# Sending turned attention features to DRAM one pipeline round later, fetching them further ahead, and a denser interleave in a two-layer linear-attention kernel

## The chip, the cores and the metric

The kernel runs on one core of a Trainium2 chip. The metric is the device time of one execution in microseconds (us). Engines are named as in the profile: PE is TensorE (PEld its weight loads), DVE is VectorE, ACT is ScalarE, POOL is GpSimd, and SP is SyncE, whose instructions here are almost all DMA issues; "SPq" is SP's instruction queue, which is worked off in order.

## The reference

Four blocks are applied in turn to x of 2048 rows by 576 columns: attention A, dense B, attention A, dense B, each with a layer norm in front and a residual around it.

```python
qkv = x @ wqkv                                   # 32 heads of 18 columns
phi_q = concat(softmax(q @ w_phi), softmax(-(q @ w_phi)))      # phi_k alike, per head
kv  = einsum("bhsf,bhsd->bhfd", phi_k, v);  z = einsum("bhsf->bhf", phi_k)
o   = einsum("bhqf,bhfd->bhqd", phi_q, kv) / (einsum("bhqf,bhf->bhq", phi_q, z) + 1e-6)
A(x) = o @ wo
B(x) = relu(x @ w1 + b1)**2 @ w2 + b2            # hidden size 4608
```

## The kernel before, in words

**Tiles.** The 2048 rows are four blocks of 512 rows, each of four row tiles t = 0..3 of 128. The hidden size is 36 slices f of 128. Every matmul operand is split into a high and a low part, and a product is three matmul groups (high by high, low by high, high by low).

**Stages of a layer.** After the key sums are known, a barrier stage computes the attention output of the first block in `order`. Then the dense part of `order[0]` runs as `g_mlp` while the attention of later blocks is woven in (first weave); then the dense part of `order[1]` runs as `g_mlp` with more attention woven in (second weave); then the last two blocks are done together by `g_pair`. In layer 0 `order` is 3, 2, 0, 1, in layer 1 it is 1, 0, 3, 2. In the profile names lose their buffer numbers: `m_3` and `m_2` are the two dense stages of layer 0, `m_1` and `m_0` those of layer 1; `a_2`, `a_0`, `a_1` and `a_3` are the attention of blocks 2, 0, 1 and 3.

**The dense stage.** For each f, `first(f)` loads a slice of w1 (tile `r1`, lines 1159 and 244) and of w2 (tile `r2`, line 1161), two buffers each, and splits them on ACT, DVE and POOL (lines 1167, 1168, 1171, 1174, 1175). `hidden(f)` (line 1190, 14 matmuls), `square(f)` (lines 1197 to 1200) and `second(f)` (lines 1217 and 1208, 15 matmuls) follow. The loop body for f issues `first(f+1)`, `hidden(f)`, `square(f)`, `second(f-1)` and then yields; with two yields ahead of the loop there are 36 yields.

**The weave.** At each yield of the dense stage, `weave` adds a rate to a credit and lets the other generator run steps while the credit is at least 1; each step yields its cost, which is taken off. So rate and costs say beside which f a step is traced. The order of tracing gives priorities only: a planner then lays down a fixed order for each engine, taking the first instruction in priority that it holds to be ready. `chained` keeps each woven step's work on DVE, ACT and POOL behind that of the step before, and `held` puts it behind the newest `square`; neither holds SP.

**The woven attention.** `g_features` makes query features: a software pipeline over t of `start`, exponential, `add`, `factors`, scaling (line 853) and `turn`. `turn` transposes tile t in blocks of 32 by 32 on DVE (line 897) and at once issues four stores to a DRAM tile (`..ft`, line 900, 144 KB each). `g_out` fetches groups of the turned features back (`fetch`, line 928, five groups of up to 504 KB; all four t must have landed), splits them (lines 941 and 942), multiplies them (line 964), multiplies by wo and adds the residual (lines 999 and 1004), and normalizes (lines 459 to 534). The first two groups are fetched right ahead of the first splitting step; each later one two groups ahead. The first weave's generator is `back_first`: features of `order[1]`, queries of `order[2]`, `g_out` of `order[1]` with the features of `order[2]` inside, and the norm of `order[1]`, whose result the second dense stage reads. The second weave's is `back_second`: `g_out` of `order[2]`, queries, features and `g_out` of `order[3]`, and a prelude for `g_pair`.

Of the kernel before, what the change touches and what calls it, by code (L numbers as in the profile page):

```python
# [15 lines left out]
NT = TB // P  # L16
# [5 lines left out]
def layers_kernel(  # L22
# [79 lines left out]
    def drain(gen):  # L102
        for _ in gen:
            pass

    def weave(main, other, rate, behind=None):

        due = 0.0
        for _ in main:
            due += rate  # L110
            while due >= 1.0:
                cost = next(other, other)
                if cost is other:
                    break
                due -= cost or 1.0
        with tc.issue_after(dense[behind]) if behind else nullcontext():
            drain(other)

    def pipeline(n, stages, costs):

        for i in range(n + len(stages) - 1):
            for k in reversed(range(len(stages))):
                if 0 <= i - k < n:
                    stages[k](i - k)
                    yield costs[k]
# [9 lines left out]
    def traced_on(engine):  # L135
        return next(i for i in reversed(nc.cur_bb.bb.instructions) if i.engine == engine.engine)

    def chained(gen, strict=False, every=False):
        ends, engines = {}, [nc.vector.engine, nc.scalar.engine, nc.gpsimd.engine]
        if every:  # L140
            engines.append(nc.tensor.engine)
        while True:
            traced = nc.cur_bb.bb.instructions
            mark = len(traced)
            if strict and not every:
                ends[nc.tensor.engine] = [traced_on(nc.tensor)]
            with ExitStack() as behind:
                for before in ends.values():
                    for ins in before:
                        behind.enter_context(tc.issue_after(ins))  # L150
                cost = next(gen, gen)
            own = {}
            for ins in traced[mark:]:
                if ins.engine in engines:
                    own.setdefault(ins.engine, []).append(ins)
            for engine, step in own.items():
                ends[engine] = step if every else step[-1:]
            if cost is gen:
                return
            yield cost  # L160
# [65 lines left out]
    dense = {"v": 0}  # L226
# [413 lines left out]
    def soft_parts(src, name, apart=False):  # L640
        if apart:
            e = sb.tile([P, 2 * D], F32R, tag="hb", name=f"{name}e").bitcast(F32)
            e = e.rearrange("p (s d) -> p s d", s=2)
        else:
            e = sb.tile([P, 2, D], F32, tag="E", name=f"{name}e", bufs=4)
        v = src.rearrange("p (h d) -> p h d", d=DH)
        mm = sb.tile([P, 2, H], F32, tag="mm", name=f"{name}m")
        nc.vector.tensor_reduce(mm[:, 0], v, op=ALU.max, axis=AX.X)
        nc.vector.tensor_reduce(mm[:, 1], v, op=ALU.min, axis=AX.X)
        e4 = e.rearrange("p s (h d) -> p s h d", d=DH)  # L650
        m = mm.unsqueeze(3).to_broadcast([P, 2, H, DH])
        dense["parted"] = nc.vector.tensor_sub(e4[:, 0], v, m[:, 0])
        dense["parted", 1] = nc.gpsimd.tensor_sub(e4[:, 1], m[:, 1], v)
        return e

    def soft_exp(e):
        return nc.scalar.activation(e, e, AF.Exp)

    def soft_sums(e, name):
        r = sb.tile([P, 2, H], F32, tag="r", name=f"{name}r", bufs=4)  # L660
        nc.vector.tensor_reduce(r, e.rearrange("p s (h d) -> p s h d", d=DH), op=ALU.add, axis=AX.X)
        nc.vector.reciprocal(r, r)
        return r
# [142 lines left out]
    def held(gen, keys=("last",)):  # L806

        while True:
            with ExitStack() as behind:
                for key in keys:  # L810
                    behind.enter_context(tc.issue_after(dense[key].ins))
                cost = next(gen, gen)
            if cost is gen:
                return
            yield cost
# [15 lines left out]
    def phi_products(layer, e, name):  # L831
        zb = sums[layer]["zb"]
        ms = [sb.tile([P, D], F32, tag="qk", name=f"{name}{s}", bufs=5) for s in range(2)]
        for s in range(2):
            (nc.gpsimd if s else nc.vector).tensor_mul(ms[s], e[:, s], zb[:, s])
        return ms

    def phi_sums(ms, name):
        u = sb.tile([P, 2, H], F32, tag="u", name=name)
        for s in range(2):  # L840
            nc.vector.tensor_reduce(u[:, s], ms[s].rearrange("p (h d) -> p h d", d=DH), op=ALU.add, axis=AX.X)
        return u

    def phi_factors(u, r):
        nc.vector.tensor_mul(u, u, r)
        nc.vector.scalar_tensor_tensor(u[:, 0], u[:, 0], DEN_EPS, u[:, 1], op0=ALU.add, op1=ALU.add)
        nc.vector.reciprocal(u[:, 1], u[:, 0])
        nc.vector.tensor_mul(r, r, u[:, 1].unsqueeze(1).to_broadcast([P, 2, H]))

    def phi_scale(e, r, which=(0, 1)):  # L850
        for s in which:
            e3 = e[:, s].rearrange("p (h d) -> p h d", d=DH)
            dense[f"scaled{s}"] = (nc.gpsimd if s else nc.vector).tensor_mul(
                e3, e3, r[:, s].unsqueeze(2).to_broadcast([P, H, DH]))
# [24 lines left out]
    def g_features(layer, raws, ph, name):  # L879

        rs, ms = {}, {}

        def start(t):
            ph.append(soft_parts(raws[t], f"{name}Q{t}"))

        def add(t):
            rs[t] = soft_sums(ph[t], f"{name}Q{t}")
            ms[t] = phi_products(layer, ph[t], f"{name}m{t}")

        def factors(t):  # L890
            phi_factors(phi_sums(ms.pop(t), f"{name}u{t}"), rs[t])

        turned[name] = home = dram.tile([2 * D, TB], F32, name=f"{name}ft")

        def turn(t):
            flat = ph[t].rearrange("p s d -> p (s d)")
            nc.vector.transpose(flat, flat)
            for i in range(NQ):
                at = t * P + 32 * i
                nc.sync.dma_start(home[:, at : at + 32].rearrange("(j f) r -> f j r", f=32),  # L900
                                  flat[32 * i : 32 * i + 32].rearrange("f (j r) -> f j r", r=32))

        yield from held(pipeline(NT, (start, lambda t: soft_exp(ph[t]), add, factors, lambda t: phi_scale(ph[t], rs[t]),
                                      turn), (2.6, 0.4, 3.0, 2.8, 1.2, 1.6)), ("last", "squared"))

    def g_out(layer, b, ph, dst, name, parts=1, pause=None, behind=None, norm=None, mid=None, costs=(None, None), o_first=None):

# [14 lines left out]
        def fetch(k):  # L922
            if k < NG:
                g, w = groups[k], gw[groups[k]]
                raws[g] = sb.tile([P, 2 * D], F32, tag="E", name=f"{name}w{g}", bufs=4)[:w, : 2 * TB]
                raws[g] = raws[g].rearrange("p (s n) -> p s n", s=2)
                src = turned[name].rearrange("(s d) n -> d s n", s=2)
                nc.sync.dma_start(raws[g], src[g * GW : g * GW + w])
# [84 lines left out]
        if parts == 1:  # L1013
            for k in range(2):
                fetch(k)
        xs_of = []
        if pause:
            product, total, factors, rescale = pause
# [41 lines left out]
        begin, scale, main, rest = next(g_norm(xs_of.__getitem__, dst, f"{name}n", None, None))  # L1060
# [760 lines left out]
    for b in range(NB - 1):  # L1821
# [6 lines left out]
              ready=lambda: qpair.extend(wpair("q", "t0", TAGS_B))))  # L1828

    order = [NB - 1, NB - 2] + list(range(NB - 2))  # L1830
    b, prev = order[0], order[1]
    x, xprev = xT[b], xT[prev]
    for layer in range(2):
        ready, raws = barrier(layer, b, prev, x, xprev, kes, vpair, qpair)
        spare["tags"] = []
        early, operands, rows, nxt, keep = [], {}, [], {}, {}
        prelude, products, seconds = g_pair(layer, order[2:], operands, rows, f"m{layer}_p")

        def back_first():
            m, later = f"a{layer}_{order[2]}", []  # L1840
            mid = (g_queries(layer, order[2], None, later, m), g_features(layer, later, early, m))
            yield from g_attend(layer, order[1], None, raws, nxt, f"a{layer}_{order[1]}", dense, None, mid)
# [80 lines left out]
                if last:  # L1923
                    keep.update(x=xk, es=es, v=wpair("v", f"w{m}"))

        weave(g_mlp(layer, order[0], ready, [], f"m{layer}_{order[0]}", dense.pop("rest")), chained(back_first()), 3.7, "rows")
        back = chained(back_second())

        def then():
            drain(back)  # L1930
            next(products)

        weave(g_mlp(layer, order[1], nxt, [], f"m{layer}_{order[1]}", None, then), back, 5.0)
        back = iter(()) if layer else chained(back_keys(), True)
        for k, _ in enumerate(products):
            if k == NP - 1:
# [6 lines left out]
        if layer == 0:  # L1943
# [18 lines left out]
            order = [b, prev] + order[:2]  # L1962
# [22 lines left out]
```

## Time and profile before

| | us |
|---|---|
| Median of 3 runs | 2440.58 (2440.19 to 2441.8) |
| The profiled execution's own time | 2441.59 |
| Its span, first to last instruction | 2439.9 |
| DVE, ACT, POOL busy | 1560.5, 1289.7, 940.6 |
| Mean granted TensorE clock | 0.998 |

Read it from the busiest engine. Where one engine is busy for nearly the whole span, the time can only fall where that engine sits idle or runs at a lower clock, so the view of its waits matters most; the order of time on the engines around such a place then says who was late, and for whom that one waited.

### The profile page before, as it was taken

What the parts mean: (1) busy time and instruction counts of PE and PEld (TensorE: products, weight loads), DVE (VectorE), ACT (ScalarE), POOL (GpSimd) and SP (SyncE); (2) the same over time, 40 slices, a digit from 0 to 9 for tenths busy, and PEclk for the clock granted to TensorE, in tenths of its full rate; (3) what the DMA queues carried; (4) which work ended last, traced back from release to release, by engine and by line L of the source; (5) the groups of instructions that cost most, each with busy time, mean ns of one, the idle gap of its engine ahead of it and who ended that gap; (6) DMA issues with size and microseconds to landing.
All of it is one profiled execution on the core that took longest, in us unless ns stands there. A gap on an engine that the chain in (4) does not pass through costs nothing. (4 is left out here: it accounts for less than half of the span.)

```text
span 2439.9 us, 41475 instructions
## 1 busy us (share of the span) xinstructions
PE 2410.0 (99%) x14806; PEld 2137.9 (88%) x14806; DVE 1560.5 (64%) x2537; ACT 1289.7 (53%) x2543; POOL 940.6 (39%) x1121
## 2 busy tenths in 40 slices
PE   9999999999999999999999999999999999999999
PEld 8999888888888888888999988888887888888898
DVE  8779847664867655545766787486557675555443
ACT  4344555444456666664443444554455466676643
POOL 4555303212335565542433442032222455565321
PEclk9999999999999999999999999999999999999999
DMA  9124573666654533338753156537667444333364
GB/s 338 64 84 165 163 194 97 151 202 220 155 173 136 157 99 115 109 104 302 257 188 139 59 173 143 168 96 186 191 233 158 141 142 145 118 103 116 110 199 130
DMA packets 370646, 379.40 MB, mean 155 GB/s; under 512 B 142886, under 2 KB 270790, under 8 KB 367878
## 3 DMA queue, kind: packets, MB, share of 16 engines
q1 hardware_dynamic: 369180, 375.37, 51.2%
q8 instruction: 116, 1.90, 0.3%
q10 hardware_dynamic: 1258, 1.37, 0.2%
q14 instruction: 92, 0.75, 0.1%
HBM read 297.22 MB, written 79.41 MB: 154 GB/s over the span
## 5 line engine op out<-in xcount | busy, mean ns | idle before, releaser
L1507 POOL TENSOR_TENSOR m_ps<-m_pr,m_ps 128x128 fp32r<-128x128 f32 x144 | 98.6, 685 | 337.8 <-ACT m_ps L1505 310.7
L1506 DVE TENSOR_TENSOR m_ps<-m_pr,m_ps 128x448 fp32r<-128x448 f32 x144 | 99.8, 693 | 175.9 <-ACT m_ps L1504 175.8
L1549 PE MATMUL m_pacc<-m_ps,m_phb 128*128 128x448 f32 x864 | 185.6, 363 | 0.0
L1549 PEld LDWEIGHTS m_pacc<-m_ps,m_phb 128*128 128x128 f32 x864 | 161.9, 188 | 15.0
L1549 PE MATMUL m_pacacc<-m_ps,m_phc 128*128 128x448 f32 x648 | 147.1, 365 | 0.0
L1504 ACT ACTIVATE m_ps<-m_pr 128x448 fp32r<-128x448 f32 x144 | 82.8, 575 | 115.7 <-issue 64.9
L1549 PEld LDWEIGHTS m_pacacc<-m_ps,m_phc 128*128 128x128 f32 x648 | 119.2, 188 | 7.7
L1190 PE MATMUL m_0ph<-a_0nh,m_0h 128*128 128x512 f32 (+1 forms) x380 | 96.7, 382 | 1.6 <-ACT m_0hr L1197 1.4
L1190 PE MATMUL m_1ph<-t1onh,m_1h 128*128 128x512 f32 (+1 forms) x380 | 96.2, 381 | 2.0 <-ACT m_1hr L1197 1.8
L1217 PE MATMUL m_2acc<-m_2s,m_2hb 128*128 128x448 f32 x432 | 95.2, 367 | 2.9 <-ACT m_2s L1168 2.6
L1190 PE MATMUL m_3ph<-t0onh,m_3h 128*128 128x512 f32 (+1 forms) x380 | 96.1, 381 | 1.8 <-ACT m_3hr L1197 1.6
L1217 PE MATMUL m_0acc<-m_0s,m_0hb 128*128 128x448 f32 x432 | 95.0, 367 | 2.9 <-ACT m_0s L1168 2.6
L1190 PE MATMUL m_2ph<-a_2nh,m_2h 128*128 128x512 f32 (+1 forms) x380 | 96.6, 382 | 0.8 <-ACT m_2hr L1197 0.6
L1217 PE MATMUL m_3acc<-m_3s,m_3hb 128*128 128x448 f32 x432 | 94.2, 364 | 2.0 <-ACT m_3hb L1198 1.4
L1217 PE MATMUL m_1acc<-m_1s,m_1hb 128*128 128x448 f32 x432 | 94.2, 364 | 2.0 <-ACT m_1hb L1198 1.4
L1217 PEld LDWEIGHTS m_2acc<-m_2s,m_2hb 128*128 128x128 f32 x432 | 81.8, 190 | 11.7 <-ACT m_2s L1168 3.0
L1217 PEld LDWEIGHTS m_0acc<-m_0s,m_0hb 128*128 128x128 f32 x432 | 81.5, 190 | 11.7 <-ACT m_0s L1168 3.0
L1217 PEld LDWEIGHTS m_3acc<-m_3s,m_3hb 128*128 128x128 f32 x432 | 80.4, 188 | 10.6 <-ACT m_3hb L1198 2.1
L1217 PEld LDWEIGHTS m_1acc<-m_1s,m_1hb 128*128 128x128 f32 x432 | 80.4, 188 | 10.5 <-ACT m_1hb L1198 2.1
L1175 POOL TENSOR_TENSOR m_3s<-m_3r,m_3s 128x128 fp32r<-128x128 f32 x36 | 22.9, 637 | 161.9 <-ACT m_3s L1169 153.3
L1175 POOL TENSOR_TENSOR m_1s<-m_1r,m_1s 128x128 fp32r<-128x128 f32 x36 | 22.8, 635 | 162.0 <-ACT m_1s L1169 151.8
L1190 PEld LDWEIGHTS m_1ph<-t1onh,m_1h 128*128 128x128 f32 x380 | 68.8, 188 | 17.4 <-ACT m_1hr L1197 3.0
(2464 smaller groups left out, 7237.0 us busy)
## 6 DMA issues: line engine op xcount, KB each, us to landing
m_pr<-in_B_w SPq DMA_DIRECT2D x144, 288.0 KB
m_pr<-in_B_w SPq DMA_DIRECT2D x72, 256.0 KB
hd<-m_pu SPq DMA_DIRECT2D x72, 256.0 KB
m_pg<-hd SPq DMA_DIRECT2D x72, 256.0 KB
m_3r<-in_B_w SPq DMA_DIRECT2D x36, 288.0 KB
m_2r<-in_B_w SPq DMA_DIRECT2D x36, 288.0 KB
m_1r<-in_B_w SPq DMA_DIRECT2D x36, 288.0 KB
m_0r<-in_B_w SPq DMA_DIRECT2D x36, 288.0 KB
```

The costliest lines, as they stand in the source:

```text
L1175: nc.gpsimd.tensor_sub(s2[:, FC + P : FC + 2 * P], r2[:, R:], s2[:, FC : FC + P].bitcast(F32))
L1190: dense["hidden"] = nc.tensor.matmul(ph[:, cols], a, m, start=(k == 0), stop=(k == len(ops) - 1))
L1217: nc.tensor.matmul(acc[t][:, :R], a[:, rows], m, start=(f == 0 and k == 0), stop=(f == NF - 1 and k == 2))
L1504: nc.scalar.activation(s2[:, RO : RO + R], r2[:, :R], AF.Copy)
L1506: nc.vector.tensor_sub(s2[:, RO + R : RO + 2 * R], r2[:, :R], s2[:, RO : RO + R].bitcast(F32))
L1507: nc.gpsimd.tensor_sub(s2[:, FC + P : FC + 2 * P], r2[:, R:], s2[:, FC : FC + P].bitcast(F32))
L1549: nc.tensor.matmul(accs[b][t][:, :R], a[:, rows], m, start=(g == 0 and k == 0), stop=(g == NF - 1 and k == 2))
```

## The change

Three things are changed. The four stores of a tile leave `turn` and become a seventh stage of the features' pipeline, `store`, with a cost of 0.2, so that tile t's are issued at the head of the next round, ahead of `turn(t+1)`; those of the last tile come after a further step of cost 4.0. In `g_out`, a step of cost 3.0 follows the first two fetches. The rates of the two weaves go from 3.7 to 3.9 and from 5.0 to 5.1. No instruction is added or removed.

```diff
         def turn(t):
             flat = ph[t].rearrange("p s d -> p (s d)")
             nc.vector.transpose(flat, flat)
+
+        def store(t):
+            flat = ph[t].rearrange("p s d -> p (s d)")
             for i in range(NQ):
                 at = t * P + 32 * i
                 nc.sync.dma_start(home[:, at : at + 32].rearrange("(j f) r -> f j r", f=32),
                                   flat[32 * i : 32 * i + 32].rearrange("f (j r) -> f j r", r=32))

-        yield from held(pipeline(NT, (start, lambda t: soft_exp(ph[t]), add, factors, lambda t: phi_scale(ph[t], rs[t]),
-                                      turn), (2.6, 0.4, 3.0, 2.8, 1.2, 1.6)), ("last", "squared"))
+        def steps():
+            yield from pipeline(NT, (start, lambda t: soft_exp(ph[t]), add, factors, lambda t: phi_scale(ph[t], rs[t]),
+                                     turn, lambda t: t < NT - 1 and store(t)), (2.6, 0.4, 3.0, 2.8, 1.2, 1.6, 0.2))
+            yield 4.0
+            store(NT - 1)
+            yield 0.2
+
+        yield from held(steps(), ("last", "squared"))
...
         if parts == 1:
             for k in range(2):
                 fetch(k)
+            yield 3.0
...
-        weave(g_mlp(layer, order[0], ready, [], f"m{layer}_{order[0]}", dense.pop("rest")), chained(back_first()), 3.7, "rows")
+        weave(g_mlp(layer, order[0], ready, [], f"m{layer}_{order[0]}", dense.pop("rest")), chained(back_first()), 3.9, "rows")
...
-        weave(g_mlp(layer, order[1], nxt, [], f"m{layer}_{order[1]}", None, then), back, 5.0)
+        weave(g_mlp(layer, order[1], nxt, [], f"m{layer}_{order[1]}", None, then), back, 5.1)
```

## The prediction, made before the changed kernel ran

> **What bounds the kernel now.** I read the page first, then the waits of PE, then the order of time on SP and DVE around the longest of them, then busy time by windows.
>
> ```profile
> span 2439.9 us, 41475 instructions
> ...
> PE 2410.0 (99%) x14806; PEld 2137.9 (88%) x14806; DVE 1560.5 (64%) x2537; ACT 1289.7 (53%) x2543; POOL 940.6 (39%) x1121
> ```
>
> PE is busy 2410.0 of 2439.9 us. The change takes no matmul away, so it can gain only from the 29.9 us of idle time and from stretches at a lower clock. PE's waits, longest first (total, times, longest):
>
> ```profile
> PE m_2acc L1217 <- ACT m_2s L1168: 2.6, 1, 2.6
> PE m_0acc L1217 <- ACT m_0s L1168: 2.6, 1, 2.6
> PE m_1ph L1190 <- ACT m_1hr L1197: 1.8, 3, 0.8
> PE m_3ph L1190 <- ACT m_3hr L1197: 1.6, 2, 0.8
> PE m_3acc L1217 <- ACT m_3hb L1198: 1.4, 1, 1.4
> PE m_1acc L1217 <- ACT m_1hb L1198: 1.4, 1, 1.4
> PE m_0ph L1190 <- ACT m_0hr L1197: 1.4, 1, 1.4
> PE a_2pn L964 <- ACT a_2fh L941: 1.1, 1, 1.1
> ```
>
> All lie in the dense stages with woven attention: m_3 and m_1 are first weaves, m_2 and m_0 second weaves. Two waits of 2.6 us are for a slice of w2 split too late (m_2s, m_0s). They cost more than they show: right behind each, the granted clock (third column from the right) falls to half for 3.4 us, which is 1.7 us of lost matmul time.
>
> ```profile
> 659.80:663.20 3.40, 3.10 (x9) 2.64 (x9) 1.03 (x2) 0.78 (x2) 1.42 (x2) 0.50 1.39 224
> ...
> 1868.10:1871.50 3.40, 3.40 (x10) 2.97 (x9) 0.63 (x1) 0.78 (x2) 0.70 (x1) 0.50 1.17 192
> ```
>
> [...] The rows show the drop after 2.6 us, so I count it.
>
> Why the slice was late, in SP's queue ahead of the first of these waits:
>
> ```profile
> 639.04 2.38 SPq L900 DMA_DIRECT2D a_1ft<-a_1Q0e  x4
> 649.43 2.33 SPq L900 DMA_DIRECT2D a_1ft<-a_1Q1e  x4
> 651.86 0.59 SPq L1161 DMA_DIRECT2D m_2r<-in_B_w  x1
> 655.15 2.30 SPq L900 DMA_DIRECT2D a_1ft<-a_1Q2e  x4
> 657.55 0.61 SPq L1161 DMA_DIRECT2D m_2r<-in_B_w  x1
> 658.25 3.26 SPq L900 DMA_DIRECT2D a_1ft<-a_1Q3e  x4
> 661.56 0.71 SPq L1159 DMA_DIRECT2D m_2r<-in_B_w  x1
> ```
> ```profile
> 638.94 0.57 DVE L1174 TENSOR_TENSOR m_2s<-m_2r,m_2s 128x448 fp32r<-128x448 f32 x1
> ...
> 648.04 1.36 DVE L897 STREAM_TRANSPOSE a_1Q1e<-a_1Q1e 128x1152 f32<-128x1152 f32 x1
> ```
>
> The w2 buffer was free at 638.94 + 0.57 = 639.5 us. Its next load went out at 651.86, 12.4 us later: SP had the stores of tile 1 ahead of it and stood at them until DVE's turn ended at 648.04 + 1.36 = 649.4. Stores that wait for DVE hold up weights that wait for nothing. SP's own waits say the same of the other places:
>
> ```profile
> SPq L900 <- DVE a_0Q1e L897: 20.4, 2, 10.7
> SPq L900 <- DVE a_2Q1e L897: 16.0, 2, 9.7
> ```
>
> And in the first weave of layer 0, where the w1 slice (L1159) was wanted:
>
> ```profile
> 288.56 1.44 DVE L1171 TENSOR_TENSOR m_3h<-m_3r,m_3h 128x640 fp32r<-128x640 f32 x1 [0.55 <-DMA m_3r<-in_B_w]
> ```
> ```profile
> 297.56 2.36 SPq L900 DMA_DIRECT2D a_2ft<-a_2Q1e  x4
> 300.02 0.58 SPq L1161 DMA_DIRECT2D m_3r<-in_B_w  x1
> 304.30 2.30 SPq L900 DMA_DIRECT2D a_2ft<-a_2Q2e  x4
> 306.64 0.66 SPq L1159 DMA_DIRECT2D m_3r<-in_B_w  x1
> ```
>
> The w1 buffer was free at 290.0, its load left at 306.64, behind tiles 1 and 2. That is 16.6 us of lead gone, over two iterations of the dense stage; the 1.4 us wait of m_3acc follows.
>
> **The change, part by part.** *The stores, one round later.* Added up from the costs, as yield of 36 before and after. First weave: turns of tiles 0 to 3 at 8, 11, 12, 13, now 8, 10, 12, 12; their stores were at the turns' yields, now 10, 12, 12, 14. Second weave: turns 15, 16, 17, 18, now 15, 17, 18, 18; stores now 17, 18, 18, 20. So tile 1's stores, the worst blockers, fall behind the weight loads of one or two further slices in the planner's priority; tile 2's hardly move (same yield as the turn); tile 3's fall two yields back. The 16 issues of about 0.6 us (2.30 to 3.26 per four) stay on SP, which has room, and are moved past the weight loads only. The tiles they read are held longer, but the next user of these buffers is the fetch, which must wait for the stores in any case: nothing new.
>
> What it is worth: both 2.6 us waits with their half clock, 2 x (2.6 + 1.7) = 8.6 us. I take all of it, since a load 12.4 us earlier leaves nothing to wait for. In the first weaves the 1.4 us waits and the 0.8 us waits (two in each layer), 1.4 + 2 x 0.8 = 3.0 us per layer: bounds 0 and 6.0, and I take half, 3.0, because tile 2's stores stay in the way.
>
> *The fetch 3.0 ahead.* It goes to yield 21 (was 19) in the second weave, its first splitting step to 21 or 22 (was 20). The two waits behind the fetch, 1.4 (m_0ph) and 1.1 (a_2pn), are ACT standing at loads that have left but not landed, at a time when the DMA engines (second column from the right) are full:
>
> ```profile
> 1850.00:1856.00 6.00, 6.00 (x29) 5.22 (x28) 6.00 (x8) 2.47 (x4) 2.98 (x2) 1.00 0.26 43
> ...
> 1872.00:1876.00 4.00, 4.00 (x20) 3.55 (x19) 1.36 (x2) 1.52 (x3) 0.75 (x1) 1.00 0.92 256
> ```
>
> While SP stood at tile 1 the share was 0.26, afterwards 0.92: the same bytes, bunched. The change spreads them. Bounds 0 and 2.5; I take half, 1.2.
>
> *The rates.* The first weave gets 12.6 units of cost more (twice 4.8 for the stores and pauses, 3.0 for the fetch) against 36 x 0.2 = 7.2 of credit. Its last norm steps move from yields 32, 33, 33, 34 to 34, 34, 35, 36: no yield is left behind the last. The second weave gets 4.8 + 2 x 3.0 = 10.8 against 3.6 and ends its prelude at 36 instead of 34; that prelude's first products come after the dense stage's epilogue, so I cost that at nothing; without that cover it is a wait for the last weight split. The first weave's end is closer:
>
> ```profile
> 496.92 0.60 PE L512 MATMUL a_2np<-ident,a_2nn 128*128 128x128 f32 x4
> ...
> 501.16 0.60 PE L512 MATMUL a_2np<-ident,a_2nn 128*128 128x128 f32 x4
> ```
>
> The last residual product ends at 496.9 and the transposes of its normalized rows start at 501.16. These 4.2 us are covered to the last by the stage's closing matmuls. The step runs this late although traced at yield 34, so moving its trace to 36 may change nothing; if the cover goes, it is up to 4.2 us and a half clock of 1.7, 5.9 per layer. A gain is excluded, since that stretch has no place in the list of waits above. Between 0 and 11.8 I take 2.0 for both layers, near the first end, by the row just named.
>
> Sum: 8.6 + 3.0 + 1.2 - 2.0 = 10.8 us. From the profiled 2441.59 that is 2430.8; the median lies 1.0 below its profiled run (2441.59 - 2440.58), so 2429.8, rounded to 2430. All listed waits and both half clocks gone, with no new cost, is 8.6 + 6.0 + 2.5 = 17.1, or 2423.5; I put the low end at 2422, since other engines' order moves as well.
>
> **The rivals.** *The stores stay where they are.* The planner goes by what it holds to be ready, not by place in the trace:
>
> ```profile
> 258.04 1.06 SPq L984 DMA_DIRECT2D a_2x<-in_A_x  x2
> ```
>
> These rows are first asked for in the norm step of yield 32, and yet were issued at 258 us, ahead of tile 1's stores at 297.56, which are traced at yield 11. If SP is free in the plan when a turn ends, its stores leave at once, whatever their priority, and the change only shifts the weave. Against it: the w1 load above, free at 290.0, was planned behind stores whose turn came later, so the planner does see a full queue there and goes by priority. Time 2440.6, give or take 2.
>
> *The transfers are the limit.* With the share at 0.92 behind the stores, loads that leave earlier may land no earlier. Then half of the 8.6 stays and the 1.2 falls away: gain 4.3 + 3.0 - 2.0 = 5.3, so 2441.6 - 5.3 - 1.0 = 2435.3. [...] Against it stands the 0.26.
>
> *The fetch takes the stores' place, and the kernel is slower.* The fetch is asked for 5.2 units after the last stores (6.6 before), and those are now the last in priority. SP then stands at the fetch until they have landed, with weight loads behind it. It decides from about 10 us of standing, what tile 1's stores show now; then each of the four weaves pays a wait such as now, 2.6 + 1.7 = 4.3, in all 17.2: 2441.6 - 10.8 + 17.2 - 1.0 = 2447. Against it: in the first weave stores and fetch lie two yields apart, and in the second the landing of the last stores took 3.32 us even among full engines, by the chain of work that ended last:
>
> ```profile
> 1868.13 3.32 DMA a_2ft<-a_2Q3e
> ```
>
>
> **How the numbers follow.** The forecast gets 0.57 (2422 to 2435), the stores staying 0.18, the transfers 0.13, the fetch 0.12. The range 2422 to 2441 holds nearly all of the first, most of the second and all of the third, about 0.8. A measurement of this kernel can tell 0.2%, 4.9 us, from no change: 2435.7 to 2445.5 is the same. Faster: 0.57 and half of the transfers, 0.64. Same: the other half and most of the second, 0.21. Slower: 0.15.
>
> **What would show it.** Right: SP's waits at L900 for a turn shrink, with the L1161 and L1159 rows ahead of the stores; the m_2s and m_0s waits of PE are gone, and no half clock near them. The second rival shows as stores in the old places among the loads; the third as a DMA share near 1 and ACT waiting for weights issued early; the fourth as a long wait at L928 with weights behind. The end of the first weave shows as a wait of the first L1190 of m_2 or m_0 for the normalized rows. I am wrong if the time is above 2436, or if the gain comes from elsewhere than the four weaves.

## The result, and the profile after

The changed kernel takes 2463.52 us (median of 4 runs, 2460.35 to 2465.5) beside 2440.67 for the kernel before on the same chip: 1.0092 times as long, 95% interval 1.0074 to 1.0109. The forecast was 2430, with 2422 to 2441 as its range. Its profiled execution took 2463.13 us. The page's head:

```profile
span 2461.4 us, 41511 instructions
...
PE 2419.7 (98%) x14806; PEld 2141.8 (87%) x14806; DVE 1566.1 (64%) x2537; ACT 1292.6 (53%) x2543; POOL 940.5 (38%) x1121
```

The span grew by 21.5 us. PE's idle time went from 29.9 to 41.7 us (11.8). Its busy time grew by 9.7 us, though it runs the same matmuls: part of the same work ran at a lower clock (mean granted clock 0.998 before, 0.996 after). Where it went, from the first matmul of each stage in both traces:

| stage | layer 0: before, after | layer 1: before, after |
|---|---|---|
| dense with first weave | 274.6, 278.9 (+4.3) | 275.1, 280.5 (+5.4) |
| dense with second weave | 297.1, 299.9 (+2.9) | 298.4, 300.2 (+1.8) |
| pair products | 316.1, 319.8 (+3.7) | 316.2, 320.4 (+4.2) |

All else together is -0.8. PE's waits after (total, times, longest); lines of the kernel stand 3 to 10 further down than before, so L900 is now L903, L928 L937, L941 L950, L1159 L1169:

```profile
PE m_ppx L1527 <- DVE m_pu L1659: 5.0, 2, 2.8
PE a_0pn L973 <- ACT a_0fh L950: 4.9, 2, 3.8
...
PE a_3pn L973 <- ACT a_3fh L950: 3.2, 1, 3.2
PE m_1ph L1200 <- ACT m_1hr L1207: 1.6, 2, 0.8
PE m_3ph L1200 <- ACT m_3hr L1207: 1.6, 2, 0.8
PE m_3acc L1227 <- ACT m_3hb L1208: 1.4, 1, 1.4
PE m_1acc L1227 <- ACT m_1hb L1208: 1.4, 1, 1.4
PE m_2ph L1200 <- ACT m_2hr L1207: 1.4, 1, 1.4
PE m_0ph L1200 <- ACT m_0hr L1207: 1.2, 1, 1.2
...
PE a_2np L512 <- DVE a_2x L1013: 0.9, 1, 0.9
```

The two 2.6 us waits for w2 are gone, as forecast, and with them the half clocks behind them. (The waits of m_2ph and m_0ph for ACT, 1.4 and 1.2, stand further on; before they were 0.6 and 1.4.) The 0.8 and 1.4 us waits of m_3 and m_1 are still in the list, as long as before. New are PE's waits for the fetched features at the start of the second weave (3.8 and 3.2, one in each layer) and for a step on the first products' accumulator at the start of the pair products (2.2 and 2.8). Windows of after around these and a third place (time, then PE, PEld, DVE, ACT, POOL busy, granted clock, DMA share, GB/s):

```profile
357.71:361.12 3.41, 2.13 (x7) 0.94 (x6) 2.50 (x4) 3.27 (x7) 0.77 (x1) 1.00 0.99 279
361.12:364.54 3.42, 3.42 (x9) 2.68 (x9) 1.60 (x3) 0.89 (x3) 0.00 (x0) 0.50 0.63 179
528.38:531.79 3.41, 0.10 (x1) 0.10 (x1) 0.64 (x1) 1.41 (x3) 0.00 (x0) 1.00 0.96 281
531.79:535.21 3.42, 3.42 (x8) 2.65 (x9) 3.32 (x6) 1.85 (x4) 0.00 (x0) 0.50 0.95 278
818.51:821.92 3.41, 1.17 (x6) 0.68 (x5) 1.95 (x4) 2.44 (x5) 2.02 (x3) 1.00 0.01 2
821.92:825.33 3.41, 3.41 (x10) 2.84 (x9) 3.41 (x10) 2.57 (x6) 0.46 (x1) 0.50 0.67 245
```

Each idle stretch of these rows is followed by 3.4 us at half clock. There are three such in each layer (in layer 1 at 1579.68, 1750.35 and 2040.48) where before had one (659.79 and 1868.10). By the clock alone that is 4 x 1.7 = 6.8 us more.

**Start of the second weave.** SP after, and two rows of SP before:

```profile
503.26 0.57 SPq L937 DMA_DIRECT2D a_0w<-a_0ft  x1
...
507.56 0.35 SPq L937 DMA_DIRECT2D a_0w<-a_0ft  x1
508.01 2.72 SPq L1288 DMA_DIRECT2D xs<-m_3x  x4
...
511.89 1.20 SPq L427 DMA_DIRECT2D a_0o0h<-wsoh  x2
...
519.34 0.38 SPq L1169 DMA_DIRECT2D m_2r<-in_B_w  x1
```
```profile
489.49 0.52 SPq L928 DMA_DIRECT2D a_0w<-a_0ft  x1
...
509.68 0.38 SPq L1159 DMA_DIRECT2D m_2r<-in_B_w  x1
```

The fifth w1 slice of the dense stage left at 519.34 in place of 509.68. Ahead of it are the last two fetches (the last at 507.56; 489.49 before), the stores of finished rows and the loads of wo, which had been spread over 20 us (489.49 to 509.68). ACT then stands at that slice:

```profile
530.38 0.74 ACT L1177 ACTIVATE m_2h<-m_2r 128x640 fp32r<-128x640 f32 x1 [4.11 <-DMA m_2r<-in_B_w]
531.03 0.61 ACT L950 ACTIVATE a_0fh<-a_0w 126x512 fp32r<-126x512 f32 x1
```

The split that PE waits for (L950) had its data; it was behind L1177 in ACT's order. PE's wait names ACT, and ACT's row names the DMA.

**Start of the pair products.** The weights of each pair of slices are split in a chain over POOL, ACT and DVE. The prelude is the split of the first pair; the splits of the second and third pair are traced with the first products. POOL's first and last step of the prelude, and first and late steps of the third pair's split, after, then before; then DVE and PE after:

```profile
784.40 1.02 POOL L1488 TENSOR_TENSOR m_ps<-m_pr,m_pr 128x384 f32<-128x384 f32 x1
...
806.87 0.53 POOL L1485 TENSOR_TENSOR m_pwb<-m_pr,m_pwb 32x128 fp32r<-32x128 f32 x1
...
811.38 1.02 POOL L1488 TENSOR_TENSOR m_ps<-m_pr,m_pr 128x384 f32<-128x384 f32 x1 [0.77 <-PE m_ppz L1527]
...
818.38 1.00 POOL L1497 TENSOR_TENSOR m_pr<-m_pr,m_ps 128x384 f32<-128x384 f32 x1
```
```profile
769.13 1.01 POOL L1478 TENSOR_TENSOR m_ps<-m_pr,m_pr 128x384 f32<-128x384 f32 x1
...
787.09 0.64 POOL L1475 TENSOR_TENSOR m_pwb<-m_pr,m_pwb 32x128 fp32r<-32x128 f32 x1
...
803.60 1.11 POOL L1478 TENSOR_TENSOR m_ps<-m_pr,m_pr 128x384 f32<-128x384 f32 x1
...
807.72 1.09 POOL L1487 TENSOR_TENSOR m_pr<-m_pr,m_ps 128x384 f32<-128x384 f32 x1
```
```profile
819.97 0.43 DVE L1483 TENSOR_TENSOR m_pwa<-m_pr,m_pwa 128x256 fp32r<-128x256 f32 x1 [2.82 <-ACT m_pwa L1482]
820.32 0.75 DVE L1659 SCALAR_TENSOR_TENSOR m_pu<-m_ppx,b1t,m_pu 128x512 f32<-128x512 f32 x1
```
```profile
817.41 1.46 PE L1227 MATMUL m_2acc<-m_2s,m_2hb 128*128 128x448 f32 x6
821.12 0.73 PE L1527 MATMUL m_ppx<-a_1nt4h,m_pwb 128*128 128x512 f32 x2 [2.24 <-DVE m_pu L1659]
```

The pair products begin 7.5 us later than before (806.3 for 798.8), but the prelude began 15.3 us later. It ended 11.1 us ahead of the first product before (787.7), and 1.1 us behind it after (807.4). The third pair's split starts at nearly the same distance from the first product in both (4.8 and 5.1 us), but after it runs among what is left of the earlier ones: its last step shown begins 7.0 us behind its first, in place of 4.1. DVE stood at a split of its result (L1483), and L1659, which frees PE's accumulator, was behind.

### The profile page after: what moved, and what is told of

It is laid out like the page before. It is cut to its first block, busy times and chain, and to the rows that moved or that the text cites. A ratio compares the mean times of both kernels' runs of the same rounds, so it can differ in the third digit from the quotient of the medians.

```text
span 2461.4 us, 41511 instructions
## 1 busy us (share of the span) xinstructions
PE 2419.7 (98%) x14806; PEld 2141.8 (87%) x14806; DVE 1566.1 (64%) x2537; ACT 1292.6 (53%) x2543; POOL 940.5 (38%) x1121
## 5 line engine op out<-in xcount | busy, mean ns | idle before, releaser
L1200 PEld LDWEIGHTS m_3ph<-t0onh,m_3h 128*128 128x128 f32 x380 | 68.8, 189 | 18.5 <-ACT m_3hr L1207 2.4
L1200 PEld LDWEIGHTS m_0ph<-a_0nh,m_0h 128*128 128x128 f32 x380 | 68.5, 190 | 16.1 <-ACT m_0hr L1207 1.6
```

Of the source, the lines that this page charges most:

```text
L1200: dense["hidden"] = nc.tensor.matmul(ph[:, cols], a, m, start=(k == 0), stop=(k == len(ops) - 1))
```

## The experiments

Times are ratios to runs of the kernel before on the same chip, as us beside 2440.7. The main theory was that the loss comes from the cost units that the change adds to the woven generators: at the rates given they let the last woven steps come 1.5 yields later in each weave, past the work that covered them. The rival was that the moved stores do it.

**e1: stores moved, without the pauses, old rates.**

```diff
-                                      turn), (2.6, 0.4, 3.0, 2.8, 1.2, 1.6)), ("last", "squared"))
+                                     turn, store), (2.6, 0.4, 3.0, 2.8, 1.2, 1.6, 0.2))
```

> The kernel before with the four stores of a tile moved to a seventh pipeline stage, also those of the last tile (one step behind its turn); no 4.0 pause, no 3.0 step after the fetch, rates 3.7 and 5.0 as before. Theory (the lost time is the added cost units, which push the tail of each weave past the work that covered it; the moved stores are good): the two 2.6 us waits for w2 and their half clocks go and none of the three new loss places appears, so 2430 to 2436 us. Rival (the moved stores themselves upset SP's queue): the new waits appear here too, 2450 to 2464 us.

1.0031 (1.0019 to 1.0043), +7.6 us: between the two ranges. None of the three new places, and the 2.6 us waits are gone, but there is no gain. PE now waits 3.9 and 4.2 us near the end of the first weaves, and 2.8 and 3.4 us for a w1 slice in the second weaves, with five windows at half clock (mean granted clock 0.997).

**e2: pauses and rates, stores in place.** Besides these lines, `yield 3.0` after the fetches and the rates 3.9 and 5.1.

```diff
-                                      turn), (2.6, 0.4, 3.0, 2.8, 1.2, 1.6)), ("last", "squared"))
+                                     turn, lambda t: None), (2.6, 0.4, 3.0, 2.8, 1.2, 1.6, 0.2))
+            yield 4.0
```

> The kernel before with its stores where they were, but with all cost units and rates of the change: 0.2 per tile and 4.0 after the features, 3.0 after the first two fetches, rates 3.9 and 5.1. Theory (cost units): the late tails appear without any moved store, about 15 us of waits and lost clock at the start of the second weave and at the start of the pair products, and the two 2.6 us waits stay: 2450 to 2465 us. Rival (the moved stores): within 4 us of 2440.

1.0077 (1.0064 to 1.009), +18.8 us: most of the 22.5, with no store moved. Its waits at the pair products are 4.5 us (5.0 in the changed kernel). Not all came as expected: the waits for the features are only 2.6 and 0.9 us, and the 2.6 us waits for w2 did not stay; 4.1 and 3.1 us for a w1 slice stand in the second weaves instead.

**e3: the change, units paid for by the rates.**

```diff
-dense.pop("rest")), chained(back_first()), 3.9, "rows")
+dense.pop("rest")), chained(back_first()), 4.08, "rows")
-None, then), back, 5.1)
+None, then), back, 5.32)
```

> The changed kernel with rates that pay for the added units in full: 4.08 in the first weave (3.7 x 136.4 / 123.8) and 5.32 in the second (5.0 x 180.8 / 170), so that the last woven steps fall on the yields of the kernel before. Theory (cost units): the waits at the start of the second weave and of the pair products go, 2432 to 2442 us. Rival (the moved stores): stays at 2455 to 2465 us.

1.002 (1.0011 to 1.003), +4.9, so 2445.6: 18 of 22.5 us are back. That lies in neither range, 4 us above the theory's and 9 below the rival's. The waits at the start of the pair products are gone. What is left lies in the first weaves (+3.4 and +3.5 us):

```profile
PE m_3acc L1227 <- ACT m_3hb L1208: 4.3, 3, 1.4
PE m_1acc L1227 <- ACT m_1hb L1208: 4.3, 3, 1.4
```

**e4: the rates alone.**

```diff
-dense.pop("rest")), chained(back_first()), 3.7, "rows")
+dense.pop("rest")), chained(back_first()), 3.9, "rows")
-None, then), back, 5.0)
+None, then), back, 5.1)
```

> The kernel before with the rates 3.9 and 5.1 alone. Theory (cost units): woven work comes up to two yields earlier, no tail is late, 2436 to 2443 us. Second rival (a denser weave by itself crowds ACT, DVE and SP): 2448 us or more.

1.0021 (1.0013 to 1.003), +5.1, so 2445.8: 3 us above the theory's range and below the rival's. Earlier is not free either.

**e5 and e6: only one weave paid,** each with one line of e3's diff: 4.08 with 5.1, and 3.9 with 5.32.

> The changed kernel with only the first weave's rate raised to pay for its added cost units, 4.08 (the second stays at 5.1). Theory (each weave's unpaid units make its own tail late): the wait at the start of the second weave goes, 3.8 us in layer 0 and 3.2 in layer 1 with 1.7 of half clock each, 10.5 in all; the wait at the start of the pair products stays, 2.2 and 2.8 us: 2450 to 2456 us. Rival (lateness runs through both weaves, the pair products' wait included, from the first): 2440 to 2448 us.

> The changed kernel with only the second weave's rate raised, to 5.32 (the first stays at 3.9). Theory (each weave's own tail): the wait at the start of the pair products goes, 2.2 and 2.8 us with 1.7 of half clock each, 8.4 in all; the wait at the start of the second weave stays: 2452 to 2458 us. Rival (it all comes from the first weave): 2460 us or more.

1.0044 (1.0032 to 1.0056) and 1.0053 (1.0038 to 1.0069): 2453.0 and 2455.1 as medians, both in the theory's range. Waits of PE in e5, then in e6:

```profile
PE m_ppx L1527 <- DVE m_pu L1659: 4.7, 2, 2.5
```
```profile
PE a_0pn L973 <- ACT a_0fh L950: 5.2, 2, 3.9
...
PE a_3pn L973 <- ACT a_3fh L950: 3.5, 1, 3.5
```

Each kernel keeps the wait of the weave that was not paid, and has lost most of the other's (in e5 the wait for L950 is 1.7 and 1.3 us). By stages, e5's pair products are as late as the change's (+3.5 and +4.4 us) and its second weaves are not (+0.2 and -3.2); in e6 the pair products are +0.1 and +1.0. The two savings, 11.8 and 9.6 us, add up to 21.4; both together (e3) gave 17.6. So each weave's tail is late by its own unpaid units.

**e7: stores issued by POOL, stores otherwise in place.**

```diff
-                nc.sync.dma_start(home[:, at : at + 32]...
+                nc.gpsimd.dma_start(home[:, at : at + 32]...
```

> The kernel before with the four stores of a tile issued by POOL instead of SP, nothing else: no store can stand ahead of a weight load in SP's queue. If the 2.6 us waits for w2 come from the stores ahead of them, as the prediction argued, they go with their half clocks: 8.6 us, 2430 to 2434 us. Rival 1 (the planner's order of other work on SP, not the stores, makes loads late; taking stores out only moves the waits): 2438 to 2450 us. Rival 2: POOL stands at the turns and its splits come late: 2445 us or more, with PE waiting for POOL's results.

1.0114 (1.0095 to 1.0133), +27.8. Rival 2's time, though not shown to be its mechanism: the 2.6 us waits are gone, and PE waits for normalized rows (3.5, 3.5, 2.7 and 2.7 us) and fetched features instead, not for POOL's results. That the waits for w2 hung on the stores fits; that freeing the loads gains time does not follow.

**e8: the 3.0 step alone; e12: 4.8 units after the features alone,** each added to the kernel before.

```diff
                 fetch(k)
+            yield 3.0
```
```diff
                                      turn), (2.6, 0.4, 3.0, 2.8, 1.2, 1.6))
+            yield 4.8
```

> The kernel before with only the 3.0 step after the first two fetches of a group, old rates. It adds 3.0 units to the first weave and 6.0 to the second (1.2 yields there). Theory (cost units): the prelude is late and PE waits at the start of the pair products, 1 to 3 us a layer and perhaps the half clock: 2443 to 2452 us, and the two 2.6 us waits stay. Rival (fetching earlier helps more than the units cost): 2436 to 2441 us.

> The kernel before with 4.8 units after the features of each block and nothing else; old rates. It adds 9.6 units to the first weave (2.6 yields) and 4.8 to the second (1.0). Theory (cost units): waits at the start of the second weave above all, 3 us or more with a half clock of 1.7 in each layer, and a smaller one at the pair products: 2450 to 2462 us. Rival: under 2445 us.

1.0027 (1.0018 to 1.0037) and 1.006 (1.0047 to 1.0073): +6.6 and +14.6, both as the theory had it in time, the places only in part. In e8 the pair products wait 1.0 us in all, there is one half clock (mean granted clock 0.999), and beside the stores 1.3 and 1.6 us (1.5 in layer 1) stand for 2.6, which was expected to stay. In e12 the loss is in the second weaves (+9.5 and +6.3 us), with 1.6 us at the first weave's last norm and seven windows at half clock in all (mean granted clock 0.995), and hardly any at the pair products; its first weaves, where 9.6 units were added, are 0.1 us longer.

**e9: all sixteen stores behind the last turn.**

```diff
+            for t in range(NT):
+                store(t)
+                yield 0.05
```

> The kernel before with all sixteen stores of a block behind the turn of its last tile, at almost no cost units, old rates. Theory (SP stands at every store whose turn is not done, and loads of weights stand behind it, whichever tile it is): SP stands once only, and the waits for weights around the stores of the second weave, 2.6 us a layer before and 2.8 to 3.4 with the stores one round later, shrink to under 1 us; 16 issues of 0.6 us in a row and a later fetch give part of it back: 2434 to 2444 us. Rival (bunching the transfers costs more than the standing): a wait of PE for the split of the fetched groups of 3 us or more in each weave, 2450 us or more.

1.0018 (1.0009 to 1.0026), +4.4: neither range. Waits for w1 beside the stores stay at 3.0 and 3.8 us; they did not shrink, and the waits of about 4 us in the first weaves are here too (4.1 and 3.9), though only 0.4 units were added there. The traced execution is the fastest of the eleven (2439.57 beside a median of 2446.11), so it does not show where the 4.4 us lie.

**e10: the changed kernel with a cheaper prelude.**

```diff
-            yield from paced(held(prelude, ("last", "squared")), 2.0)
+            yield from paced(held(prelude, ("last", "squared")), 1.0)
```

> The changed kernel with the seven steps of the prelude at 1.0 unit each in place of 2.0, nothing else. Theory (the prelude's place beside the last dense slices is what makes the pair products wait): the waits at the start of the pair products go, 2.2 and 2.8 us with 1.7 of half clock each, 8.4 in all: 2453 to 2458 us. Rival (the whole second weave is late, and the prelude's pace does not matter): 2460 to 2465 us.

1.0078 (1.0065 to 1.009), 2459.4: between. The waits at the pair products are gone, as the theory said (their stage is +0.1 and +0.7 us), and 6.5 us are lost in the second weaves in exchange (+6.0 and +5.2, where the change had +2.9 and +1.8). (Its first weaves are 2.6 and 1.6 us shorter than the change's; its mean granted clock is 0.997, the change's 0.996.) The prelude's lateness was the cause of that wait; pressing it into the same yields only moved the price.

**e11: the change in the second weaves only, paid in full.** The new stage, the pauses and the 3.0 hang on a flag that is set between the two weaves; rates 3.7 and 5.32.

```diff
+            if in_second:
+                yield 3.0
```

> The change in the second weaves only, paid in full (rate 5.32); the first weaves as in the kernel before (stores at the turn, no added units, 3.7). Theory (what is left of the loss once the units are paid lies in the first weaves, about 2 to 3.5 us each): 2437 to 2443 us. Rival (the first weave was only the place where it showed): 2445 us or more.

0.9995 (0.9986 to 1.0004): as the theory had it, no loss and no gain that can be told.

**e13 to e16: residual rows' stores issued by POOL,** on the kernel before, e1, e9 and e11.

```diff
-            nc.sync.dma_start(xm[b][t], x)
+            nc.gpsimd.dma_start(xm[b][t], x)
```

> The kernel before with the stores of the residual rows (xm) issued by POOL, behind POOL's own addition, in place of SP, where they waited 82 us in all for that addition. Theory (SP's standing costs only where a load of weights with little lead is behind it; the kernel before has no such place at these stores): 2437 to 2444 us. Rival (every standing of SP costs): under 2435 us.

> The store move alone with the residual rows' stores issued by POOL. In the store move alone, SP stood 7.2 us at one of them in each first weave with the load of a w1 slice behind it, and PE waited 3.9 and 4.2 us with half clocks. Theory (that standing is what the moved stores had become in the first weaves): those waits go, about 11 us: 2437 to 2442 us; the waits for w1 behind the turned stores in the second weaves stay. Rival (moving the stores costs for another reason): 2446 us or more.

> All sixteen stores behind the last turn, and the residual rows' stores issued by POOL. It had the same two waits of 3.9 and 4.1 us in the first weaves. Theory: they go, 2434 to 2438 us. Rival: 2443 us or more.

> The change in the second weaves only, paid in full, and the residual rows' stores issued by POOL. It had no wait at these stores' place. Theory: 2437 to 2442 us. Rival (every standing of SP costs): under 2435 us.

1.0013 (1.0004 to 1.0022), 1.0042 (1.0029 to 1.0054), 1.0014 (1.0005 to 1.0023) and 0.9992 (0.9983 to 1.0001). e13 is at the upper end of the theory's range (its median, 2444.73, 0.7 above) and e16 in it; e14 and e15 came out in their rivals'. In e14 the waits of about 4 us in the first weaves went, and others of nearly the same size came at the end of the same stages:

```profile
PE a_2po L1005 <- DVE a_2nl L521: 3.7, 1, 3.7
...
PE a_0po L1005 <- DVE a_0nl L521: 3.1, 1, 3.1
```

Taking SP's standing away there did not bring e1's loss back, so that theory fell. Left to suspect were the 0.2 units that e1 added to each tile.

**e17: e1 with the 1.6 of the turn split, so that nothing is added; e18: the change with 4.4 in the first weave.**

```diff
-                                     turn, store), (2.6, 0.4, 3.0, 2.8, 1.2, 1.6, 0.2))
+                                     turn, store), (2.6, 0.4, 3.0, 2.8, 1.2, 1.55, 0.05))
```

> The store move alone with no added cost units at all: the turn's 1.6 is split into 1.55 for the turn and 0.05 for the store (in the store move alone each tile cost 0.2 more, 1.6 units in the first weave or 0.4 yields). Theory (the move itself replaces one wait by another): 2446 to 2452 us as with the 0.2, with a wait of some 3 us for w1 beside the last tiles' stores in each second weave. Rival (even 0.4 yields of lateness made the loss of the move): 2432 to 2442 us.

> The changed kernel with 5.32 in the second weave and 4.4 in the first, 8% more than pays for the added units. Theory (what is left in the first weaves with the units paid, about 2 us each, is not lateness; a denser weave does not take it away): 2444 to 2452 us. Rival (the first weaves are still late): 2438 to 2443 us.

e17: 0.9999 (0.999 to 1.0008), the rival. So 1.6 units in a first weave (0.4 yields) and 0.8 in a second (0.2) made the difference of 7.8 us, and the move itself is worth nothing either way. That they did it by lateness is not shown: e9, with 0.1 yields, has the same waits in its first weaves, and a small change of costs also changes the planner's order. e18: 1.0008 (0.9999 to 1.0017), a median of 2443.2, on the rival's edge. It is 2.9 us below e3, but the two intervals overlap, so that the rest in the first weaves is lateness stays a hint.

**All together.** The delay of the last woven steps follows from the units ahead of them over the rate, less the same for before (123.8 / 3.7 = 33.5 yields in the first weave, 170 / 5.0 = 34.0 in the second). The change adds 13.0 and 11.0 units:

| kernel | delay, first and second weave (yields) | us over before |
|---|---|---|
| e7, stores issued by POOL | 0, 0 | 27.8 |
| the change | 1.6, 1.5 | 22.5 |
| e10, cheaper prelude | 1.6, 0.1 | 19.0 |
| e2, stores in place | 1.5, 1.5 | 18.8 |
| e12, 4.8 units alone | 2.6, 1.0 | 14.6 |
| e6, second paid | 1.6, 0 | 12.9 |
| e5, first paid | 0.1, 1.5 | 10.7 |
| e14, e1 and rows' stores by POOL | 0.4, 0.2 | 10.2 |
| e1, move with 0.2 a tile | 0.4, 0.2 | 7.6 |
| e8, 3.0 alone | 0.8, 1.2 | 6.6 |
| e4, rates alone | -1.7, -0.7 | 5.1 |
| e3, both paid | 0.1, 0 | 4.9 |
| e9, all stores last | 0.1, 0 | 4.4 |
| e15, e9 and rows' stores by POOL | 0.1, 0 | 3.4 |
| e13, rows' stores by POOL | 0, 0 | 3.2 |
| e18, first overpaid | -2.4, 0 | 2.0 |
| e17, move at no cost | 0, 0 | -0.2 |
| e11, second weaves only, paid | 0, 0 | -1.2 |
| e16, e11 and rows' stores by POOL | 0, 0 | -2.0 |

Leaving e7 aside, the kernels that are 0.2 yields or more late in a weave lost 6.6 us or more, the others 5.1 or less. Among the late ones the order is not that of the delays, and the others differ by 7 us with no lateness at all: an edit also changes the planner's order, and a few us either way cannot be put down to a delay. What is shown is the large part: the units alone make 18.8 of the 22.5 us (e2), and paying for them takes 17.6 away (e3), weave by weave (e5, e6).

## Why the prediction was wrong

**The rates.** This is the step that failed. The prediction counted the units (12.6 against 7.2 of credit, 10.8 against 3.6; with the last `yield 0.2` of each block's features, which it left out, 13.0 and 11.0) and the two yields of delay, and then gave the tails almost no price, 2.0 us in all, because of what would cover them. By e5 and e6 they cost 11.8 + 9.6 us. Of the 33.5 us between forecast and result about half is this; the rest is gain that did not come: paid for, the change was still to gain 12.8 us (8.6 + 3.0 + 1.2) and lost 4.9 (e3).

For the second weave it said "I cost that at nothing; without that cover it is a wait for the last weight split". What came is close to that: 2.24 + 2.80 us and two half clocks at the start of the pair products, 8.4 us by the trace, 9.6 by e6, a wait for an accumulator that DVE frees behind a weight split. The cover named, the dense stage's epilogue, did not lie ahead of the first products: they ran first, from 806.3, and the wait began at 818.9, right behind the epilogue's own matmuls (817.41 + 1.46). What the products need is that the splits are done by then. In the trace of before the prelude ended 11.1 us ahead of the first product; that lead was there to be read, and the delay used it up.

**The first weave's end** was given 2.0 us, between 0 and 11.8. At the place named, the transposes of the normalized rows, there are 0.9 us in each layer. The price came 27 us later, where the lateness had bunched fetches, stores and loads on SP ahead of a w1 slice: 3.83 + 3.24 us and two half clocks, 10.5 us by the trace, 11.8 by e5. The list of what is late next ended one step too early. Tails have a queue behind them.

**The stores** were to bring 8.6 for the w2 slices. Moved alone they bring 0 (within 2.4), by e17. The step "since a load 12.4 us earlier leaves nothing to wait for" was wrong. SP, DVE and PE in e17, where the stores come one round later at no cost:

```profile
643.56 0.58 SPq L1167 DMA_DIRECT2D m_2r<-in_B_w  x1
651.50 2.33 SPq L903 DMA_DIRECT2D a_1ft<-a_1Q1e  x4
...
657.22 2.30 SPq L903 DMA_DIRECT2D a_1ft<-a_1Q2e  x4
660.56 2.31 SPq L903 DMA_DIRECT2D a_1ft<-a_1Q3e  x4
662.91 0.64 SPq L1165 DMA_DIRECT2D m_2r<-in_B_w  x1
```
```profile
644.36 0.98 DVE L1177 TENSOR_TENSOR m_2h<-m_2r,m_2h 128x640 fp32r<-128x640 f32 x1
```
```profile
PE m_0ph L1196 <- ACT m_0h L1173: 2.8, 1, 2.8
PE m_2ph L1196 <- ACT m_2h L1173: 2.1, 1, 2.1
```

The w2 slice of the prediction now leaves at 643.56, ahead of tile 1's stores, 8.3 us earlier than in before, and the wait for it is gone. The next w1 slice leaves at 662.91, behind the stores of tiles 1, 2 and 3, though its buffer was free at 644.36 + 0.98 = 645.3. It had left just so in before, at 661.56, in a row that the prediction quotes: that lateness stood ready behind the wait for w2, and PE now pays for it (2.1 and 2.8 us). In the full change tile 1's stores left 12.5 us later than in before, and the same w1 slice, with a buffer free at 654.2, stood behind tiles 1 and 2:

```profile
661.93 3.60 SPq L903 DMA_DIRECT2D a_1ft<-a_1Q1e  x4
667.46 2.30 SPq L903 DMA_DIRECT2D a_1ft<-a_1Q2e  x4
669.81 0.64 SPq L1169 DMA_DIRECT2D m_2r<-in_B_w  x1
```

There PE waited only 0.45 us for that slice (0.58 in layer 1), so at this place the changed kernel has the gain that was forecast, and it paid elsewhere. In the versions traced that leave the stores on SP, four sets of them, each waiting for its turn, take the same stretch of SP's queue, and a load of w1 is behind them in each case shown: at 661.56 in before, at 662.91 in e17, at 669.81 in the changed kernel.

The 3.0 us taken for the first weaves did not come either. The 1.4 us wait of m_3acc ended with ACT's square (L1198), not with a load: ACT's relu and square of that slice, 0.69 and 0.63 us, make up nearly all of it. If the late w1 slice that the prediction put ahead of it was behind it, then through the order that the planner chose, and no run shows that. In the changed kernel this wait is gone from its place (318.9) and one of the same length stands at 479.1; the 0.8 us waits, which end with a relu, are as many as before. (The prediction's list of waits also leaves out the longest in total, 4.4 us for the first weights at the program's start, outside the dense stages; nothing in the change touches it.)

Nor is it shown that the half clocks, 3.4 of the 8.6, would have come back in time: of 106 executions of before, three had a mean clock of 1.000, and took 2441.71, 2441.76 and 2442.51 us, beside a median of 2441.4.

So the planner did move the stores, against the rival that they stay; its time, 2440.6, is nevertheless what the move alone gives. The rival of the transfers as the limit forecast a smaller gain, not a loss; the DMA share at the new waits is 0.96 in one and 0.01 in the other, so it does not tell.

**The fetch ahead** was given +1.2. With its units unpaid it cost 6.6 (e8); paid for, in the second weaves of e11 with the rest, it and the later stores together bring under 0.2%. In the changed kernel the 1.1 us wait of a_2pn in layer 1 is gone, but in the first weaves, where the step stands too, PE waits 0.8 and 1.1 us at the fetched features, each time with a half clock behind it (at 361 us above). The rival of the fetch taking the stores' place forecast 2447 by another mechanism, SP standing at the fetch; that was not seen.

**What stays open.** With everything paid (e3) 4.9 us remain, in the first weaves, and with rates alone (e4) 5.1. The traces of before and of the changed kernel show waits of 1.44 and 0.78 us that repeat to the hundredth (1.4 and 0.8 us in the lists of e3 to e6): the first where PE's fixed order brings `second` directly behind its own `square`, the second where `hidden` comes directly behind the one before it. In e3 there are three of 1.4 us in each first weave for one before. What makes the planner choose that order was not tried. No version is faster than the kernel before by more than can be told: the best, e16, is 0.9992 with 1.0001 inside its interval.

## What to carry to other kernels

Where costs and rates place work beside other work, a step that is given a cost moves everything behind it: work out the shift at the tail in yields, and read from the trace of before how much lead the tail has, at the end of each stage and one queue further. Here 13 and 11 units that the rates did not pay for cost some 18 us, and the moved stores by themselves nothing. Before crediting an instruction that is moved out of a load's way, look for the next load behind the rest of its kind in that queue.

## What the runs showed of the hardware

In the traces of before and of the changed kernel the half clocks come on a raster. The granted clock is 0.50 for 3.41 us from 659.79 and 1868.10 us in before, and from 361.12, 531.79, 821.92, 1579.68, 1750.35 and 2040.48 in the changed kernel (and once more in each in its last 2 us). The two of before are 1208.31 us apart, 354 times 3.4133 us; those of the changed kernel begin 0, 50, 135, 357, 407 and 492 times that length behind its first.

In windows of that length, laid from these starts through both traces from 20 us on, PE's idle time in the window right ahead of these half clocks was 2.57 and 2.02 us in before and 1.28, 3.31, 2.24, 1.58, 2.40 and 2.80 us in the changed kernel. The largest that were not followed by one are 1.44 and 1.36 us in before (from 318.46 and 1878.35) and twice 1.44 us in the changed kernel (from 477.17 and 1695.73), more than the 1.28 us beside the products of fetched features (357.71 above) that were. All 2.57 us of before's wait for w2 in layer 0 lay in one window. In e17 a longer wait, 2.77 us, stands as 1.07 and 1.70 in the first two of these rows, and the clock stayed at 1.00:

```profile
1868.30:1871.72 3.42, 2.35 (x12) 1.79 (x10) 0.00 (x0) 0.00 (x0) 0.00 (x0) 1.00 1.02 186
1871.72:1875.13 3.41, 1.71 (x7) 1.43 (x8) 1.45 (x2) 1.51 (x3) 0.55 (x1) 1.00 0.91 279
1875.13:1878.54 3.41, 3.18 (x14) 2.21 (x12) 1.29 (x2) 1.15 (x2) 0.10 (x1) 1.00 1.08 259
```

So a wait of 2.57 us brought a half clock, 1.7 us of matmul time, and one of 2.77 us none. That its place on the raster decides is an estimate from these rows; no run shows it. How much of a half clock stays in the kernel's time is open, by the three executions of before named above.
